# Three of six hidden pairs by seven products in each of chunks 3 to 6, with the sums placed early and one buffer for loaded values

## The chip, the cores and the metric

One core of a Trainium2 chip runs the whole program. The metric is the device time of one execution in microseconds. The kernel before takes 328.5 us (median of 3 runs, 328.02 to 328.99).

The profile names the engines PE (TensorE, matmuls), PEld (TensorE's weight loads), DVE (VectorE), ACT (ScalarE), POOL (GpSimd) and SP (SyncE, which here only issues transfers). The granted clock is the share of TensorE's full clock that the profile shows as allowed. A bank is one of the pieces of PSUM, the memory into which TensorE writes. An L and a number is a line of the kernel's source. The line numbers of the two kernels differ, so I pair lines by what they do.

## The reference, cut to what matters

```python
# attention over keys and values that are means of 8 neighbours: 8 batches, 8 heads, 576 rows, 64 columns
k_p = k.reshape(B, H, 72, 8, 64).mean(axis=3)
v_p = v.reshape(B, H, 72, 8, 64).mean(axis=3)
attn = softmax(q @ k_p.T / 8)
x = (attn @ v_p) as 4608 tokens x 512
# gated block
gate = maximum(x @ w_gate, 0)          # 512 -> 1536
out = (gate * (x @ w_val)) @ w_out     # 1536 -> 512
```

## The kernel before

The attention of batch c + 1 is woven between the products of chunk c of 512 tokens; there are nine chunks, 0 to 8. GpSimd adds up the means (the code calls these additions trees) two batches ahead, and issues the loads.

An ordinary hidden block computes 128 gates and 128 values for 512 tokens:

```python
def gate_val(c, fo, t0=0, n=TCH):          # 4 + 4 matmuls of 128x512
    ...
    nc.scalar.activation(out=relu[:, :n], in_=ps[0][:, :n], func=AF.Relu)
    nc.vector.tensor_tensor(out=h_tiles[c][:, fo, t0:t0 + n], in0=ps[1][:, :n], in1=relu[:, :n], op=ALU.mult)
```

Two such blocks, fo and fo + 6, and the two halves of the chunk form a 2 x 2 block product, which can be done with seven products instead of eight (28 matmuls of 256 columns instead of 16 of 512). The price is sums of weights, sums of inputs and more additions behind the products. The kernel before does this for two pairs of chunk 6, all six of chunk 7 and four of chunk 8. The output product already uses seven products in each chunk.

The parts on GpSimd that the argument touches:

```python
vin_pool = ctx.enter_context(tc.tile_pool(name="vin", bufs=2))

def prep_k(b, load_next, behind=None):
    for i in range(KJ // 2):
        run(pool_k(b, i, nc.gpsimd))                       # trees of keys
    if behind is not None:
        nc.gpsimd.tensor_copy(out=gate, in_=behind)        # holds the loads back
    if load_next:
        load_k(b + 1); load_q(b + 1); load_v(b + 1)

def prep_v(b):
    for g in range(NG):
        run(pool_v(b, g, nc.gpsimd))                       # trees of values
```

The queries are transposed by a DMA that SyncE issues when they have landed.

The softmax here doesn't subtract the row's maximum and nothing guards it: scores larger than these inputs give would overflow.

Of the kernel before, what the change touches and what calls it, by code (L numbers as in the profile page):

```python
# [16 lines left out]
def kernel(  # L17
# [13 lines left out]
    POOL = 8  # L31
# [15 lines left out]

    KP = 12
# [9 lines left out]
    vin_pool = ctx.enter_context(tc.tile_pool(name="vin", bufs=2))  # L58
    tree_pool = ctx.enter_context(tc.tile_pool(name="tree", bufs=2))
# [7 lines left out]
    relu_pool = ctx.enter_context(tc.tile_pool(name="relup", bufs=3))  # L67
    fout_pool = ctx.enter_context(tc.tile_pool(name="foutp", bufs=2))
    pexp_pool = ctx.enter_context(tc.tile_pool(name="pexpp", bufs=2))
# [19 lines left out]
    kg = const_pool.tile([P, QT * 2 // POOL, 2 * D], F16, name="kg")  # L89
    warm_sb = const_pool.tile([P, TCH], F16, name="warm_sb")  # L90


    stats = [const_pool.tile([P, NG, 4 * D], F16, name=f"stat{i}") for i in range(2)]
# [58 lines left out]
    def load_v_wide(b):  # L152
        tl = vin_pool.tile([P, H, POOL, D], F16, name="v_in")
        main = tl[:, :H // 2].rearrange("p h t d -> p (h t d)").rearrange(
            "p (h t d) -> p h t d", h=H, d=D)
        rest = tl[:P // 2, H // 2:].rearrange("p h t d -> p (h t) d")[:, :H]
        v_tiles[b] = (main, rest)
        nc.gpsimd.dma_start(
            out=main.rearrange("p h t d -> p h (t d)"),
            in_=v[b].rearrange("h (x t) d -> x h (t d)", t=KG)[:P])  # L160
        nc.gpsimd.dma_start(
            out=rest, in_=v[b].rearrange("h r d -> r h d")[P * KG:])
# [34 lines left out]
    def pool_v(b, g, eng):  # L197
        st = stats[b % 2][:SP, g, :].rearrange("p (x d) -> p x d", d=D)[:, 0::3, :]
        src = v_tiles[b][:SP, 2 * g:2 * g + 2].rearrange("p h t d -> p h (t d)")
        return tree(eng, SP, src, st)  # L200
# [135 lines left out]
    def pool_v_array(b, half):  # L336

        ps = ps_mm.tile([P, HH, D], F32, name="mm_ps", tag="mm_ps")
        main, rest = v_tiles[b]
        hs = slice(half * HH, (half + 1) * HH)  # L340
        for t in range(KG):
            nc.tensor.matmul(
                out=ps[:SP], lhsT=sel_main, rhs=main[:, hs, t, :], start=(t == 0), stop=False)
        nc.tensor.matmul(
            out=ps[:SP], lhsT=sel_rest[:P // 2], rhs=rest[:, hs, :], start=False, stop=True)
        g0 = half * NG // 2
        st = stats[b % 2][:SP, g0:g0 + NG // 2, :]
        st = st.rearrange("p g (x d) -> p g x d", d=D)[:, :, 0::3, :]
        src = ps[:SP].rearrange("p (g x) d -> p g x d", x=2)
        nc.scalar.copy(st, src)  # L350
# [6 lines left out]
    def piece_scores(t):  # L357
        n, j = divmod(t, 2)
        cols = [(j, n * IQ, IQ)] if n < NF else [(0, NF * IQ, RI), (1, NF * IQ, RI)]
        e = pexp_pool.tile([P, H, P], F16, name="pexp")  # L360
# [15 lines left out]
    def values(b, t):  # L376
# [6 lines left out]
        for half in range(2):  # L383
            ps = ps_at.tile([P, 512], F32, name="at_ps", tag="at_ps")
            for h in range(half * HH, (half + 1) * HH):
                g, hh = divmod(h, 2)
                c0 = g % (NG // 2) * W + hh * (D + 1)
                s0 = 3 * D - 1 if hh else 0
                nc.tensor.matmul(  # L389
                    out=ps[:n, c0:c0 + D + 1], lhsT=weights(b, h, t),  # L390
                    rhs=stats[b % 2][:SP, g, s0:s0 + D + 1], start=True, stop=True,
                )
# [73 lines left out]
    def out_rows(c, ts, eng=None):  # L466
# [3 lines left out]
        def part(lo, hi):  # L470
# [8 lines left out]
            if hi == n_fo:  # L479
                o = fout_pool.tile([P, DM], F32, name="fout")  # L480
# [13 lines left out]
    wo_sums = const_pool.tile([P, 4, n_hf, HD], F16, name="wo_sums")  # L494

    def weight_sums():
# [3 lines left out]
        t1, t2, t3, t4 = [wo_sums[:, i] for i in range(4)]  # L500
        return [lambda o=o, x=x, y=y, i=slice(i, i + 2): nc.vector.tensor_tensor(
                    out=o[:, i], in0=x[:, i], in1=y[:, i], op=ALU.subtract)
                for o, x, y in ((t1, f, e), (t2, h, t1), (t3, h, f), (t4, g, t2))
                for i in range(0, n_hf, 2)]

    def out_products(c, last=False):
# [5 lines left out]
        S = [sum_pool.tile([P, n_hf, HT], F16, name=f"sum{i}") for i in range(4)]  # L512
        e, g, h = wo_sb[:, :n_hf, :HD], wo_sb[:, n_hf:, :HD], wo_sb[:, n_hf:, HD:]
        T = [wo_sums[:, i] for i in range(4)]
# [72 lines left out]
    def last_products(c):  # L587
# [5 lines left out]
        S = [sum_pool.tile([P, n_hf, HT], F16, name=f"sum{i}").rearrange(  # L593
            "p f (z t) -> p f z t", z=2) for i in range(4)]
        e, g, h = wo_sb[:, :n_hf, :HD], wo_sb[:, n_hf:, :HD], wo_sb[:, n_hf:, HD:]
        T = [wo_sums[:, i] for i in range(4)]
# [83 lines left out]
    F_HALF = n_hf * P  # L680
    w_sums, x_sums, mids = {}, {}, {}

    def hidden_weight_sums():

        flat = [vin_pool.tile([P, H, POOL, D], F16, name="v_in").rearrange(
            "p h t d -> p (h t d)") for _ in range(2)]
        flat.append(kin_pool.tile([P, KJ, POOL, D], F16, name="k_in").rearrange(
            "p j t d -> p (j t d)"))
        n = N_CO * F_HALF
        views = [t[:, i * n:(i + 1) * n] for t in flat for i in range(2)]  # L690
        views += [q16_pool.tile([P, QT * D], F16, name="q16")[:, :n] for _ in range(2)]
        views = [t.rearrange("p (k f) -> p k f", k=N_CO) for t in views]
        w_sums[0], w_sums[1] = views[:4], views[4:]
        for f0 in range(0, F_HALF, 2 * P):
            fs, fu = slice(f0, f0 + 2 * P), slice(F_HALF + f0, F_HALF + f0 + 2 * P)
            for m, w in enumerate((wg_sb, wv_sb)):
                s1, s2, s3, s4 = [t[:, :, fs] for t in w_sums[m]]
                a11, a12 = w[:, :N_CO, fs], w[:, N_CO:, fs]
                a21, a22 = w[:, :N_CO, fu], w[:, N_CO:, fu]
                for o, x, y, op in ((s1, a21, a22, ALU.add), (s2, s1, a11, ALU.subtract),  # L700
                                    (s3, a11, a21, ALU.subtract), (s4, a12, s2, ALU.subtract)):
                    nc.gpsimd.tensor_tensor(out=o, in0=x, in1=y, op=op)

    def x_quarters(c):
        x0 = c * TCH % RING
        return [x_T[:, k * N_CO:(k + 1) * N_CO, x0 + t * HT:x0 + (t + 1) * HT]
                for k in range(2) for t in range(2)]

    def x_sums_of(c):

        e, f, g, h = x_quarters(c)
        x_sums[c] = [exp_pool.tile([P, 2, HS], F16, name="expT").rearrange(
            "p x s -> p (x s)")[:, :N_CO * HT].rearrange("p (k t) -> p k t", k=N_CO)
            for _ in range(4)]
# [5 lines left out]
    def take_mids():  # L720
# [4 lines left out]
        tiles += [fout_pool.tile([P, DM], F32, name="fout") for _ in range(2)]  # L725
# [3 lines left out]
    def hidden_products(c, fo, z):  # L729
# [28 lines left out]
        def summed(i):  # L758
            return lambda m: w_sums[m][i][:, :, fs]
# [56 lines left out]

    def hidden_round(c, fo, others, sums):
# [28 lines left out]
    def prep_k(b, load_next, behind=None):  # L846

        for i in range(KJ // 2):
            run(pool_k(b, i, nc.gpsimd))
        if behind is not None:  # L850
            nc.gpsimd.tensor_copy(out=gate, in_=behind)  # L851
        if load_next:
            load_k(b + 1)
            load_q(b + 1)
            load_v(b + 1)

    def prep_v(b):
        for g in range(NG):
            run(pool_v(b, g, nc.gpsimd))
# [10 lines left out]
    def attention(b):  # L870
# [10 lines left out]
        return [[kt]] + [[]] * (b + 1 < B) + trios + [[p] for p in V], []  # L881

# [7 lines left out]
    with tc.manual_schedule():  # L890
# [95 lines left out]
        load_v(2)  # L986

# [16 lines left out]
        prep_k(2, True)  # L1004
        prep_v(2)
# [4 lines left out]
        for c in range(1, n_chunks):  # L1010
            gv = [lambda fo=fo: gate_val(c, fo) for fo in range(n_fo)]

            if c == 1:
                sums = weight_sums()
                units = weave_units(gv[:-1], o[5:])
            elif c < C_HIDDEN:
                prods, sums = out_products(c - 1)
                units = []
                order = range(n_fo - 1)
                if c == C_HIDDEN - 1:  # L1020

                    order = [fo for fo in range(n_fo) if fo % n_hf > 1]
                for fo in order:
                    if c == C_HIDDEN - 1 and len(prods) == 2:
                        units.append(gv[fo])
                        continue
                    units.append(gv[fo])
                    if prods and fo not in (1, 4, 7, 10):
                        units.append(prods.pop(0))
# [31 lines left out]
            prep_v_at = 3  # L1061
            if c + 1 < B:
                others, later = attention(c + 1)
                if left:
                    others[1:2] = [[piece] for piece in left]
# [5 lines left out]
            for i, unit in enumerate(units):  # L1071
                if i == 3 and c + 2 < B:
                    prep_k(c + 2, c + 3 < B, h_tiles[c][:, 1, :1] if c > 1 else None)
                if i == prep_v_at and c + 2 < B:
                    prep_v(c + 2)
                unit()
                if c == 1:
                    run(sums[i:i + 1])
# [6 lines left out]
                if c == C_HIDDEN - 1 and i == 0:  # L1085
                    hidden_weight_sums()
                elif c == C_HIDDEN - 1 and i == 11:
                    run(x_sums_of(c))
            if c == C_HIDDEN - 1:
                take_mids()  # L1090
                more = x_sums_of(c + 1)
                run(hidden_round(c, 0, prods, sums[6:] + more[:2]) + more[2:])
            else:
                gv[-1]()
# [32 lines left out]
```

## Time and profile before

| what | before |
|---|---|
| time | 328.5 us |
| TensorE busy | 97% of the span |
| VectorE, GpSimd, ScalarE busy | 69%, 63%, 47% |
| a matmul of 512, of 256 columns, back to back | 0.216 us, 0.109 us |
| lost by TensorE over the span | 17.4 us: 9.5 before the second chunk, 3.8 in chunks 1 to 8, 4.1 behind them |

"Lost" in this document always means the same thing. I take how much later each matmul starts than the one before it, subtract the usual spacing for its width (216 ns for 512 columns, 123 for 288, 109 for 256, 56 for 128, 32 for 65 and so on), and add this up over a stretch. In contrast to "busy" it also counts time in which a matmul stands in the queue and seems to run. Stretches are cut where a chunk transposes its pooled keys, once a chunk. The lines of the profile of before are shown in the prediction.

### The profile page before, as it was taken

Reading aid. Unit: us, or ns where it says so; the run is one execution under the profiler, and the core shown is the slowest. Engines: PE = TensorE matmul, PEld = TensorE weight load, DVE = VectorE, ACT = ScalarE, POOL = GpSimd, SP = SyncE. Lnnn points to the kernel's source line nnn. Section 1 sums busy time; section 2 is a strip of 40 time slices with the busy share of each in tenths; the row PEclk is TensorE's granted clock in tenths of the full one; section 3 lists DMA queues with packets and bytes.
Section 4 is the critical chain, followed back from the end, with each engine's and each line's share of the span. In section 5 each row is a group of like instructions: output and inputs, shape, how many; then the busy total and the mean of one; then the engine's idle time right before and its main releaser. Section 6 shows DMA issues by size and latency. Waiting matters only on the chain.

```text
span 326.5 us, 6890 instructions
## 1 busy us (share of the span) xinstructions
PE 316.8 (97%) x2614; PEld 224.7 (69%) x2614; DVE 226.6 (69%) x482; ACT 151.9 (47%) x353; POOL 206.2 (63%) x258
## 2 busy tenths in 40 slices
PE   7899999999999999999999999999999999999995
PEld 2577885455566656665888866655667888888674
DVE  7465737677684864696387745784789989879762
ACT  1444482364466226612672257225925565565331
POOL 8556607999999942992199309999902577667300
PEclk9999999999999999999999999999999999999999
DMA  7999998996958539953694472123012220130044
GB/s 111 187 201 204 200 213 148 197 171 123 187 105 159 103 98 149 170 85 89 139 165 82 86 113 51 32 49 123 1 26 50 41 90 0 25 110 0 12 116 132
DMA packets 51009, 35.44 MB, mean 109 GB/s; under 512 B 30432, under 2 KB 45024, under 8 KB 50976
## 3 DMA queue, kind: packets, MB, share of 16 engines
q0 software_dynamic: 18304, 18.88, 35.8%
q1 hardware_dynamic: 32528, 16.00, 22.5%
q8 instruction: 20, 0.33, 0.4%
q10 hardware_dynamic: 144, 0.13, 0.1%
q14 instruction: 13, 0.11, 0.1%
HBM read 37.75 MB, written 9.44 MB: 145 GB/s over the span
## 4 chain that ended last, share of the span: by engine, by line
PE 88%; DVE 6%; DMA 2%; issue 1%; ACT 1%; POOL 1%; DVEq 0%; ACTq 0%; POOLq 0%
PE mm_ps L430 42%; PE acc_ps L530 19%; PE mm_ps L749 9%; PE at_ps L310 4%; PE mm_ps L475 3%; PE at_ps L389 3%; PE mm_ps L609 2%; PE at_ps L749 2%; DMA q<-in_q_dram 2%; DVE px L395 1%; DVE sum L521 1%; DVE h L439 1%; PE mm_ps L412 1%; DVE px L765 1%; PE mm_ps L284 1%
## 5 line engine op out<-in xcount | busy, mean ns | idle before, releaser
L439 DVE TENSOR_TENSOR h<-mm_ps,relu 128x512 f16<-128x512 f32 (+1 forms) x96 | 59.8, 624 | 68.2 <-PE mm_ps L430 55.2
L436 ACT ACTIVATE relu<-mm_ps 128x512 f16<-128x512 f32 (+1 forms) x96 | 52.2, 544 | 99.9 <-PE mm_ps L430 91.7
L430 PE MATMUL mm_ps<-x_T,wv_sb 128*128 128x512 f16 (+1 forms) x432 | 88.5, 332 | 0.3 <-DVE kpT0u L266 0.3
L430 PE MATMUL mm_ps<-x_T,wg_sb 128*128 128x512 f16 (+1 forms) x432 | 88.5, 332 | 0.0
L430 PEld LDWEIGHTS <-wv_sb 128*128 128x128 f16 x432 | 42.2, 98 | 31.1 <-DVE kpT0u L266 0.8
L430 PEld LDWEIGHTS <-wg_sb 128*128 128x128 f16 x432 | 40.0, 98 | 20.7 <-issue 0.4
L327 ACT ACTIVATE expT<-at_ps 72x288 f16<-72x288 f32 (+2 forms) x128 | 39.7, 384 | 13.4 <-PE at_ps L310 12.7
L530 PEld LDWEIGHTS <-sum 128*128 128x128 f16 x336 | 32.3, 98 | 6.8 <-DVE sum L521 1.2
L395 DVE TENSOR_TENSOR px<-at_ps,prd 128x256 f16<-128x256 f32 (+1 forms) x80 | 33.8, 423 | 2.7
L183 POOL TENSOR_TENSOR tree_b<-tree_a 72x256 f32<-72x256 f32 (+1 forms) x42 | 33.1, 789 | 3.3
L771 POOL TENSOR_TENSOR h<-px 128x256 f16<-128x256 f16 x36 | 25.5, 720 | 13.4 <-ACT px L768 12.3
L530 PE MATMUL acc_ps<-wo_sums,sum 128*128 128x256 f16 x252 | 31.0, 273 | 0.0
L177 POOL TENSOR_TENSOR tree_a<-v_in 72x512 f32<-72x512 f16 x24 | 28.7, 1194 | 0.1
L177 POOL TENSOR_TENSOR tree_a<-k_in 96x512 f32<-96x512 f16 x18 | 20.9, 1160 | 12.1 <-DMA k_in<-in_k_dram 12.1
L530 PEld LDWEIGHTS <-h 128*128 128x128 f16 x252 | 24.0, 98 | 3.0
L851 POOL COPY gate<-h 128x1 f16<-128x1 f16 x4 | 1.5, 381 | 36.8 <-DVE h L439 36.8
L770 POOL TENSOR_SCALAR px<-px 128x256 f16<-128x256 f16 x12 | 13.0, 1080 | 18.3 <-PE mm_ps L749 15.2
L530 PE MATMUL acc_ps<-wo_sb,h 128*128 128x256 f16 x168 | 20.6, 273 | 0.0
L521 DVE TENSOR_TENSOR sum<-h 128x768 f16<-128x768 f16 x28 | 19.3, 689 | 0.0
L538 DVE TENSOR_TENSOR rows<-acc_ps,mid 128x512 f32<-128x512 f32 x21 | 14.4, 686 | 4.8 <-PE acc_ps L530 4.6
L389 PEld LDWEIGHTS <-expT 72*128 72x128 f16 (+1 forms) x280 | 12.9, 100 | 5.9 <-DVE prd L394 0.8
L394 DVE RECIPROCAL prd<-at_ps 128x4 f32<-128x4 f32 (+1 forms) x80 | 13.7, 171 | 3.7 <-PE at_ps L389 3.6
(144 smaller groups left out, 520.2 us busy)
## 6 DMA issues: line engine op xcount, KB each, us to landing
out_dram<-rows SPq DMA_DIRECT2D x24, 256.0 KB
k_in<-in_k_dram POOLq DMA_DIRECT2D x7, 576.0 KB, 6.7
q<-in_q_dram POOLq DMA_DIRECT2D x7, 576.0 KB, 8.9
v_in<-in_v_dram POOLq DMA_DIRECT2D x6, 576.0 KB, 12.6
out_dram<-rows SPq DMA_DIRECT2D x14, 128.0 KB
wg_sb<-in_moe_w_gate_dram POOLq DMA_DIRECT2D x6, 256.0 KB, 11.4
wv_sb<-in_moe_w_val_dram POOLq DMA_DIRECT2D x6, 256.0 KB, 11.0
wo_sb<-in_moe_w_out_dram POOLq DMA_DIRECT2D x3, 512.0 KB, 10.1
```

The lines of the kernel that those rows point to most:

```text
L177: eng.tensor_tensor(out=cell["a"][:n], in0=src[:, :, :4 * D], in1=src[:, :, 4 * D:], op=ALU.add)
L183: eng.tensor_tensor(out=cell["c"][:n], in0=a[:n, :, :2 * D], in1=a[:n, :, 2 * D:], op=ALU.add)
L327: nc.scalar.activation(out=out_ap, in_=in_ap, func=AF.Exp, scale=EXP_SCALE)
L389: nc.tensor.matmul(out=ps[:n, c0:c0 + D + 1], lhsT=weights(b, h, t), rhs=stats[b % 2][:SP, g, s0:s0 + D + 1], start=True, stop=True,)
L395: nc.vector.tensor_tensor(out=x[:n, half * NG // 2:(half + 1) * NG // 2, :, :], in0=pv.rearrange("p g (x c) -> p g x c", x=2)[:, :, :, :D] ...
L430: nc.tensor.matmul(out=t[:, lo:hi], lhsT=w[:, ci, fsl], rhs=x_T[:, ci, x0:x0 + hi - lo], start=(ci == 0), stop=(ci == n_co - 1),)
L436: nc.scalar.activation(out=relu[:, :n], in_=ps[0][:, :n], func=AF.Relu)
L439: nc.vector.tensor_tensor(out=h_tiles[c][:, fo, t0:t0 + n], in0=ps[1][:, :n], in1=relu[:, :n], op=ALU.mult)
L521: nc.vector.tensor_tensor(out=S[k][:, i], in0=x[:, i], in1=y[:, i], op=op)
L530: nc.tensor.matmul(out=ps[:, tb, :], lhsT=lhs[:, i, tb * P:(tb + 1) * P], rhs=rhs[:, i, :], start=(first and tb == 0 and i == 0), stop=(tb ...
L749: nc.tensor.matmul(out=ps[key][:, m], lhsT=w_of(m)[:, i], rhs=xs[:, i], start=(first and m == 0 and i == 0), stop=(m == 1 and i == N_CO - ...
L771: nc.gpsimd.tensor_tensor(out=hc[:, fo_out, cols], in0=gv[:, 0], in1=gv[:, 1], op=ALU.mult)
```

## The change

Its intent is to take columns off TensorE: in chunks 3 to 6 three of the six pairs go by seven products, the first three of each chunk's pairs, all behind the values. Chunk 6 did two pairs so before, so ten pairs are new. The order of each chunk is now a written string. To make room for the sums of weights, values have one load buffer instead of two. The trees' intermediate tiles (one instead of two), the sums of the output product (three tiles instead of four) and the row buffers are shared more tightly as well; no run tests these apart, but a tree of keys starts every 2.44 us as before. The sums of the output product move to the beginning of a chunk. The diff is cut.

```diff
-    vin_pool = ctx.enter_context(tc.tile_pool(name="vin", bufs=2))
+    vin_pool = ctx.enter_context(tc.tile_pool(name="vin", bufs=1))
...
+    E_PAIRS = 3
+    C_EARLY = 3
+    def early_weight_sums():                 # six sums of 128x768 on GpSimd, ahead of chunk 1
...
+    EARLY_ORDER = """
+        X X g s S kt K o s S q g s a o s X a g s a o s X a g s s a
+        o a v g v o v T g v o v
+        x1 x5 y1 x2 x6 y5 x3 y2 x7 y6 z1 x4 y3 z5 y7 z2 z6 y4 z3 z7 o z4 W"""
...
+            elif key == "K":
+                if c == C_HIDDEN - 1:
+                    hidden_weight_sums()     # eight sums of 128x768 on GpSimd, in chunk 6
+                if c < C_EARLY:
+                    trees_k(b + 1)
+                    trees_v(b + 1)
+                if b + 2 < B:
+                    nc.gpsimd.tensor_copy(out=gate, in_=h_tiles[c][:, ...])
+                    load_k(b + 2); load_q(b + 2); load_v(b + 2)
+            elif key == "T":                 # trees of keys
+                trees_k(b + 2)
+            elif key == "W":                 # trees of values
+                trees_v(b + 2)
```

In the string, g is an ordinary block, o an output product, s a sum for it, X a sum of inputs, a three scores, v a piece of values, kt the transposes of pooled keys, q those of queries, S the sending of a result, and x1 to z7 the seven products of the three pairs. Behind each pair's products ScalarE takes relus and GpSimd makes the products of gate and value (three a pair, 128x256). T stands before the pairs, so the trees of keys stand ahead of these products in GpSimd's queue.

## The prediction

> **What bounds the kernel now.** First the page's engine totals:
>
> ```profile
> span 326.5 us, 6890 instructions
> PE 316.8 (97%) x2614; PEld 224.7 (69%) x2614; DVE 226.6 (69%) x482; ACT 151.9 (47%) x353; POOL 206.2 (63%) x258
> PEclk9999999999999999999999999999999999999999
> ```
>
> TensorE is busy nearly throughout at full granted clock. Busy is not the same as full speed, so I next read the chain of waits in order of time (start us, length us, what), in the fourth and sixth chunks of 512 tokens (chunks 3 and 5 in the code's count from 0):
>
> ```profile
> 131.47 1.73 PE mm_ps L430 x8
> 133.57 1.31 PE acc_ps L530 x12
> ...
> 216.39 1.39 DVE sum L521
> 217.79 0.60 DVE rows L538
> 218.39 0.84 DVE sum L521
> ```
>
> Eight matmuls of 512 columns take 1.73 us, 0.216 us each; twelve of 256 columns take 1.31 us, 0.109 us each. A column costs the same either way. Summing over the trace how much later each matmul starts than the usual spacing of its width allows, I find from 30 us to 303 us about 5.5 us of lost time (1.67 us to 58, 0.44 in chunk 1, 1.06 in chunk 2, 0.20, 0.24, 0.69 and 0.62 in chunks 3 to 6, 0.57 in chunk 7). So the kernel is bound by the number of columns streamed. What interrupts it is short: at 216 to 219 us the last product of the output waits for its sum on VectorE, and the same happens at 116 us.
>
> Next the windows, one a chunk for chunks 2 to 6, then chunk 7, which already computes all pairs by seven products (columns: window, length, busy us and instructions of each engine, clock, DMA share, GB/s):
>
> ```profile
> 82.00:118.80 36.80, 36.45 (x276) 22.30 (x273) 27.17 (x60) 16.41 (x35) 33.85 (x44) 1.00 0.70 128
> 118.80:152.40 33.60, 33.60 (x245) 20.93 (x243) 22.51 (x45) 14.81 (x32) 19.11 (x25) 1.00 0.69 121
> 152.40:186.30 33.90, 33.90 (x326) 28.84 (x324) 22.67 (x45) 14.80 (x32) 19.23 (x25) 1.00 0.61 120
> 186.30:220.30 34.00, 33.69 (x260) 22.28 (x259) 22.05 (x45) 14.80 (x32) 23.75 (x25) 1.00 0.35 66
> 220.30:255.20 34.90, 34.82 (x269) 23.17 (x267) 26.22 (x54) 18.59 (x54) 18.96 (x17) 1.00 0.18 47
> 255.20:303.00 47.80, 47.77 (x434) 42.24 (x433) 41.61 (x72) 28.52 (x66) 32.81 (x41) 1.00 0.15 45
> ```
>
> VectorE (third busy figure) has 11 us to spare in chunks 3 to 5, ScalarE 19 us, GpSimd 10 to 14 us. Chunk 7 shows that 87% of VectorE can be carried with little stall if the order suits.
>
> **What the Trainium skill says.** "Perfetto Trace Analysis", section "Identifying the Most-Contended Engine", warns that matmul busy time does not tell how near TensorE is to its limit; hence the spacing above. "TensorE: Matmul & The Clock Gate", section "Back-to-back issue gap", gives N/2.4 + 2.5 ns for an isolated gap, which this trace meets (216 and 109 ns), and 131 ns sustained at 512 columns, which it does not. "SBUF — State Buffer", section "SBUF: two separate sides", says that a VectorE operation with two SBUF inputs and a GpSimd operation that reads SBUF exclude each other for a whole instruction. The trace agrees: a 128x768 sum takes 0.55 us with GpSimd idle (124.7 us) and up to 1.98 us beside a tree (130.6 us).
>
> **The change part by part.**
>
> TensorE. A pair of hidden blocks (one of the first six and its partner), gate and value, is now 16 matmuls of 512 columns: 16 x 0.216 = 3.46 us. By seven products it is 28 of 256 columns: 28 x 0.109 = 3.05 us, so 0.41 us less a pair. Three pairs in each of chunks 3 to 6 are twelve, but two of chunk 6 were done so before: ten new pairs. The built programs confirm 444 instead of 556 matmuls of 512 columns and 1596 instead of 1412 of 256: 112 x 0.216 - 184 x 0.109 = 4.14 us less. (Chunk 4 wraps round the ring of inputs and already runs in 256-column halves, so its saving is real but made of other counts.) No other matmul count changes. This is all on the path: **-4.1 us**.
>
> VectorE, per pair: two products of 128x512 from PSUM (0.69 us each, 1.38) become three additions (0.68) and one product of 128x256 (0.42), 2.46 us; plus 1.08. Per chunk 3 x 1.08 and four input sums (0.42 to 0.89 each, say 2.3) make +5.5 us: 28 us of a chunk that should take 32.5, or 87%. This lies beside TensorE, but unevenly. Taking the new order row by row, everything before the pairs (six ordinary blocks 4.1, eight sums 6.3, input sums 2.3, five values of 1.2 each, four output additions 2.75) is 21.5 us of VectorE against 21.9 us of TensorE. With GpSimd's trees now beside the sums it can be 2 us more. I expect VectorE to be 2 to 3 us behind when the pairs begin, with the values waiting for their three banks.
>
> ScalarE, per pair: two relus of 0.60 become three copies of 0.59, three relus of 0.41 and one of 0.38: 3.4 us, so 10.1 us for three pairs against 10.5 us of TensorE in that stretch (21 products of 0.437 and one output product of 1.31). Locally that is full. The copies wait for four row buffers that VectorE's additions release, so VectorE's lag passes on. I estimate about 1 us of new stall per chunk where values and pairs follow each other, in four chunks: **+4 us**.
>
> GpSimd. Six sums of 128x768 come in before chunk 1. It has an idle hole there:
>
> ```profile
> 50.38 1.14 POOL L177 TENSOR_TENSOR tree_a<-k_in 96x512 f32<-96x512 f16 x1 [12.12 <-DMA k_in<-in_k_dram]
> ...
> 128.19 0.45 POOL L851 COPY gate<-h 128x1 f16<-128x1 f16 x1 [10.28 <-DVE h L439]
> ```
>
> From 0.72 us for 256 f16 elements and about 1.2 for 512, 768 should take about 1.7 us; six are 10.2 us, which fit into the 12.1 us. Later, each of chunks 3 to 6 gets nine products of 0.72, 6.5 us, within its spare time. In chunk 6 the 24 weight sums of about 1.2 us (29 us, spread over chunks 5 and 6) become eight of about 1.7 (14 us).
>
> One buffer for values instead of two: a load can only start after the trees of the batch before. The loads land 6 us (keys), 8 (queries) and 11 to 12 us (values) after the issue of the keys, so mostly it hides behind trees of keys (about 8 us). Following GpSimd with measured durations: trees of batch 4 end at 108 us instead of 110, then the loads of batch 5 land (114 us), trees of 5 to 132, loads of 6 land at 139, its key trees end at 146.5. The first of the nine products of chunk 3 is wanted at about 145 us and its buffer at 147. So chunk 3 may lose about 1 us there, **+1 us**. In chunk 4 the corresponding trees end at about the same time as the first product is ready.
>
> Sums early in a chunk remove the two waits at 117 and 218 us (0.5 us each), and interleaving takes some of the 0.62 us of chunk 6 and of chunk 2's 1.06: **-1.5 us**. Start and tail keep their products; their 7.8 and 4.1 us of gaps stay.
>
> Sum: 328.5 - 4.1 + 4 + 1 - 1.5 = 327.9. The two positive terms are my least certain; the order looks tuned, and any pause of TensorE lets VectorE catch up. I take 1 us off: **327.0 us**.
>
> **The rivals.**
>
> First, the column count decides alone: 324.4 us, and with the old waits gone, 323. For it: chunk 7 at 87% VectorE loses 0.57 us in 48 us. Against it: there the load is even, while here both VectorE and ScalarE are full in turns.
>
> Second, VectorE becomes the bound of chunks 3 to 6. If contention makes its sums 1.0 us on average, its 28 us become 30, and each chunk stays at 33.5 to 34.5 us: total 328 to 331. For it: sums of 1.3 to 2.0 us beside trees. Against it: 30 is still under 32.5.
>
> Third, the single value buffer or GpSimd's order (trees of keys ahead of the products, values behind) holds back the hidden blocks, and the next chunk's first sum and product wait: 3 to 6 us in chunk 3, perhaps again in chunk 4, total 330 to 335. For it: GpSimd is 92% busy in chunk 2 and has no double buffer left. Against it: its 10 us of waiting at the gate is slack before anything is late.
>
> Fourth, a gain beyond 2%, that is under 321.9 us: it needs the whole 4.1 us and 2.5 of the 5.5 us of old stalls with no new ones.
>
> **Range and chances.** The column saving is certain within 0.2 us. New stalls between nothing and twice my 5 us, less up to 1.5 us of old ones, give 322.9 to 332.9; I narrow the upper end a little: 323.0 to 332.0. Faster by over 2% (under 321.9) 0.05, slower by over 2% (over 335.1) 0.04, within 0.91.
>
> **What would show it.** TensorE's matmul spacings must stay 0.216 and 0.109 us, with 2686 matmuls. My steps are right if chunk 3 to 6 windows are 33 to 34 us each, VectorE is busy 27 to 30 us in each, values and pairs show gaps on TensorE ended by VectorE or ScalarE, and GpSimd's six early sums end before 51 us. Chunks of 32.3 us without gaps mean that rival one holds and my stall term was wrong. A wait of VectorE's additions or of the first sum of a chunk for GpSimd above 2 us means rival three. A changed start (before 30 us) or tail would be outside all this.

## The result, and the profile after

The changed kernel takes 342.84 us (median of 4 runs, 340.76 to 344.58) against 328.26 us of the kernel before beside it. The ratio is 1.0439, 95% interval 1.0369 to 1.051: slower by 4.4%, outside my range. A ratio here is the mean time of one kernel's fast runs over that of the other's of the same rounds, so not quite the ratio of the medians that I quote.

The engine totals of the page after:

```profile
span 340.0 us, 7128 instructions
PE 319.0 (94%) x2686; PEld 233.2 (69%) x2686; DVE 253.9 (75%) x517; ACT 170.9 (50%) x405; POOL 222.2 (65%) x275
PEclk9999999999999999999899999999999999999999
```

TensorE fell to 94% of a longer span, no other engine is near its limit, and in one slice of forty the granted clock is lower. So nothing became the bound as a whole; the loss must be local. The windows of chunks 3 to 6, cut at the chunks' own beginnings (columns as in the prediction):

```profile
123.65:164.55 40.90, 34.78 (x280) 25.33 (x279) 28.88 (x57) 19.52 (x45) 28.85 (x39) 0.96 0.75 125
164.55:198.85 34.30, 33.35 (x329) 29.18 (x328) 27.42 (x56) 20.21 (x47) 25.62 (x34) 1.00 0.75 118
198.85:233.15 34.30, 33.22 (x281) 24.48 (x280) 27.28 (x56) 20.21 (x47) 16.91 (x22) 1.00 0.37 67
233.15:270.40 37.25, 33.99 (x281) 24.46 (x280) 33.47 (x56) 21.64 (x63) 21.05 (x18) 1.00 0.20 45
```

Chunks 4 and 5 take 34.3 us, just above the 33 to 34 that I expected. Chunk 3 takes 40.9 and has the mean granted clock of 0.96; chunk 6 takes 37.25, with VectorE busy for 33.5 us in it instead of the 28 that I had worked out for an ordinary chunk of the four. Split by loss, in us:

| stretch | lost before | lost after | change |
|---|---|---|---|
| start to the second chunk | 9.51 | 10.46 | +0.95 |
| chunk 1 | 0.44 | 0.04 | -0.40 |
| chunk 2 | 1.06 | 2.09 | +1.03 |
| chunk 3 | 0.20 | 8.66 | +8.46 |
| chunk 4 | 0.24 | 1.99 | +1.75 |
| chunk 5 | 0.68 | 2.08 | +1.40 |
| chunks 6 to 8 | 1.20 | 5.53 | +4.33 |
| behind chunk 8 | 4.09 | 4.13 | +0.04 |

The changes add up to +17.6 us. The columns at their usual spacing fell from 307.93 to 303.80 us, that is by 4.13 us. The spans differ by 17.56 - 4.13 = 13.4 us (326.5 and 340.0). So the gain is there in full, and new stalls have eaten it four times over. There are three places: chunk 3, chunk 6, and about 1.5 us in each of chunks 4 and 5.

**Chunk 3.** The chain of waits in order of time (start, length, what) of the changed kernel, through that chunk:

```profile
144.12 6.27 DMA k_in<-in_k_dram
...
150.47 1.15 POOL tree_a L183
...
157.36 0.11 POOL kp L194
...
157.77 1.30 POOL h L893 x2
...
159.10 0.70 DVE relu L889
...
159.84 2.32 PE mm_ps L871 x11
```

Before, this stretch of the chain was nearly all TensorE's. Now the chain runs from a load of keys, through GpSimd's trees of them, to GpSimd's first product of a gate and a value (h), from there to an addition on VectorE, which waited 5.63 us for the relu buffer that this product frees, and only then to TensorE. TensorE's own line at the end of it (start, busy time, and in brackets the idle time before it and what ended it):

```profile
159.84 0.40 PE L871 MATMUL mm_ps<-early_x,wg_sb 128*128 128x256 f16 x2 [5.04 <-DVE relu L889]
```

The gap costs more than its 5 us. The windows behind it:

```profile
159.80:161.50 1.70, 1.66 (x9) 1.23 (x9) 0.92 (x2) 1.03 (x4) 1.15 (x2) 0.58 0.15 58
161.50:164.20 2.70, 2.70 (x18) 2.05 (x16) 1.48 (x3) 0.66 (x2) 1.96 (x3) 0.63 0.00 0
```

The granted clock is 0.58 and 0.63 over these 4.4 us: 1.70 x 0.42 + 2.70 x 0.37 = 1.7 us more, as an estimate. The two windows average over their edges: from 160.1 to 163.4 us alone the clock is 0.50. The Trainium skill, "TensorE: Matmul & The Clock Gate", section "HAM oscillation — how this bites in real kernels", names gaps over about 3.4 us as the ones to avoid because the clock falls. This trace agrees: after the 5 us gap the clock fell, while the gaps under 1 us elsewhere left it at 1.00. But a gap of that length is not needed. In the run below that reorders the pairs, the clock was 0.50 from 96.6 to 100.0 us, after three waits of 0.81, 0.28 and 0.49 us within 2.5 us.

Why GpSimd came so late shows on its own timeline, where the waits stand in brackets:

```profile
84.25 1.14 POOL L183 TENSOR_TENSOR tree_a<-v_in 72x512 f32<-72x512 f16 x1 [4.80 <-DMA v_in<-in_v_dram]
...
115.42 0.86 POOL L136 DMA_DIRECT2D v_in<-in_v_dram  x1
120.58 1.14 POOL L183 TENSOR_TENSOR tree_a<-k_in 96x512 f32<-96x512 f16 x1 [4.30 <-DMA k_in<-in_k_dram]
133.21 1.15 POOL L183 TENSOR_TENSOR tree_a<-v_in 72x512 f32<-72x512 f16 x1 [4.62 <-DMA v_in<-in_v_dram]
144.12 0.56 POOL L131 DMA_DIRECT2D k_in<-in_k_dram  x1
150.47 1.15 POOL L183 TENSOR_TENSOR tree_a<-k_in 96x512 f32<-96x512 f16 x1 [4.11 <-DMA k_in<-in_k_dram]
157.77 3.17 POOL L893 TENSOR_TENSOR h<-relu 128x256 f16<-128x256 f16 x5
```

Four waits for loads, all on one engine that works in order. Between the first and the second it does not pause, yet the gate before the loads of batch 5 comes at 114 us. I had expected 108. The values issued at 115.42 land at 133.1, 17.7 us later, although those of the kernel before took 12.4 (issued at 98.97, landed at 111.38). The five products at 157.77 run back to back; the first two of them held TensorE.

**Chunks 4 and 5.** The chain in chunk 5 of the changed kernel, cut:

```profile
217.43 0.25 PE at_ps L395 x8
...
224.61 1.90 DVE relu L889 x3
...
227.60 0.43 DVE h L926
```

The wait for a late sum, which stood in the chain before at 216 to 219 us, is gone. In its place VectorE's work for the pairs (L889 the addition of two products, L926 the product of a gate and a value) stands in the chain twice where the pairs begin.

**Chunk 6.** VectorE's sums for the output there (of the changed kernel; the pair of numbers at the front is start and busy time of both):

```profile
235.93 3.30 DVE L529 TENSOR_TENSOR sum<-h 128x768 f16<-128x768 f16 x2
239.75 3.31 DVE L529 TENSOR_TENSOR sum<-sum,h 128x768 f16<-128x768 f16 x2
```

That is 1.65 us for a sum that takes 0.55 alone. What GpSimd did at the same time:

```profile
235.08 1.82 POOL L732 TENSOR_TENSOR k_in<-wg_sb 128x768 f16<-128x768 f16 x1
...
238.77 1.96 POOL L732 TENSOR_TENSOR k_in<-wg_sb 128x768 f16<-128x768 f16 x1
```

The eight sums of weights for chunk 7 run one after another from there. So a sum on VectorE takes about as long as one of GpSimd's sums beside it. The prediction quotes the skill on such pairs of operations.

### The profile page after: what moved, and what is told of

The parts are those of the page before. It is cut to its first block, busy times and chain, and to the rows that moved or that the text cites. A ratio compares the mean times of both kernels' runs of the same rounds, so it can differ in the third digit from the quotient of the medians.

```text
span 340.0 us, 7128 instructions
## 1 busy us (share of the span) xinstructions
PE 319.0 (94%) x2686; PEld 233.2 (69%) x2686; DVE 253.9 (75%) x517; ACT 170.9 (50%) x405; POOL 222.2 (65%) x275
## 4 chain that ended last, share of the span: by engine, by line
PE 77%; DVE 10%; POOL 6%; DMA 4%; issue 1%; ACT 1%; POOLq 0%; DVEq 0%
PE mm_ps L436 29%; PE acc_ps L538 16%; PE mm_ps L783 8%; PE mm_ps L871 7%; PE at_ps L316 3%; PE mm_ps L481 3%; PE at_ps L395 2%; PE mm_ps L619 2%; DVE sum L529 2%; POOL tree_a L183 2%; DVE relu L889 2%; DMA k_in<-in_k_dram 2%; DMA q<-in_q_dram 2%; POOL tree_b L189 2%; DVE px L401 1%
## 5 line engine op out<-in xcount | busy, mean ns | idle before, releaser
L445 DVE TENSOR_TENSOR h<-mm_ps,relu 128x512 f16<-128x512 f32 (+1 forms) x76 | 45.8, 604 | 36.9 <-PE mm_ps L436 29.7
L442 ACT ACTIVATE relu<-mm_ps 128x512 f16<-128x512 f32 (+1 forms) x76 | 40.2, 530 | 64.6 <-PE mm_ps L436 55.9
L436 PE MATMUL mm_ps<-x_T,wg_sb 128*128 128x512 f16 (+1 forms) x328 | 67.9, 332 | 0.0
L436 PE MATMUL mm_ps<-x_T,wv_sb 128*128 128x512 f16 (+1 forms) x328 | 67.8, 332 | 0.0
L893 POOL TENSOR_TENSOR h<-relu 128x256 f16<-128x256 f16 x36 | 24.5, 697 | 38.4 <-ACT relu L892 38.4
L436 PEld LDWEIGHTS <-wv_sb 128*128 128x128 f16 x328 | 32.0, 98 | 23.7 <-DVE kpT0u L272 0.4
L885 ACT COPY row<-mm_ps 128x512 f32<-128x512 f32 x36 | 19.5, 589 | 15.4 <-PE mm_ps L871 15.4
L889 DVE TENSOR_TENSOR relu<-mm_ps,row 128x512 f16<-128x512 f32 x24 | 16.1, 686 | 10.1 <-POOL h L893 5.6
L538 PE MATMUL acc_ps<-wo_sb,sum 128*128 128x256 f16 x168 | 21.4, 278 | 1.7 <-DVE mid L546 0.9
L538 PE MATMUL acc_ps<-wo_sums,sum 128*128 128x256 f16 x168 | 20.8, 272 | 0.2 <-DVE sum L529 0.2
L538 PE MATMUL acc_ps<-wo_sb,h 128*128 128x256 f16 x168 | 20.6, 273 | 0.0
L395 PEld LDWEIGHTS <-expT 72*128 72x128 f16 (+1 forms) x280 | 13.4, 100 | 7.4 <-DVE px L401 1.1
```

The costliest lines, as they stand in the source:

```text
L436: nc.tensor.matmul(out=t[:, lo:hi], lhsT=w[:, ci, fsl], rhs=x_T[:, ci, x0:x0 + hi - lo], start=(ci == 0), stop=(ci == n_co - 1),)
L538: nc.tensor.matmul(out=ps[:, tb, :], lhsT=lhs[:, i, tb * P:(tb + 1) * P], rhs=rhs[:, i, :], start=(first and tb == 0 and i == 0), stop=(tb ...
L893: nc.gpsimd.tensor_tensor(out=hc[:, fo_out, cols], in0=gv[key][:, 0], in1=gv[key][:, 1], op=ALU.mult)
```

## The experiments

The theories: the order of GpSimd's queue (trees of keys ahead of the products of the pairs) makes the gap of chunk 3; against it, the late loads and the single buffer make it, whatever the order. The weight sums in chunk 6 make the second loss; against it, chunk 6 suffers from what came before. Every run computed the right result. Runs of one group shared a chip and the runs of the kernel before. Some executions of several variants were 2 to 6% slower than the fastest of the same kernel; they count as slow and are in no ratio.

### Trees of keys behind the pairs

```diff
-        o a v g v o v T g v o v
-        x1 x5 ... z3 z7 o z4 W
+        o a v g v o v g v o v
+        x1 x5 ... z3 z7 o z4 T W
```

> Only the order on GpSimd changes: in chunks 3 and 4 the trees of the keys stand behind the nine products of the pairs instead of ahead of them. Theory A (the products of chunk 3 wait in GpSimd's queue behind trees that themselves wait for a load): the 5.2 us gap of TensorE at 154.5 us and the low clock after it (0.58 to 0.63 from 159.8 to 164.2 us) go, chunk 3 loses about 2 us like chunks 4 and 5 instead of 8.7, and the time is 335 to 337.5 us against 342.8 for the changed kernel. Theory B (VectorE and ScalarE are too full where values and pairs meet, my step of +4 us): chunk 3 keeps most of its loss and the time stays above 340 us.

335.8 us median (fast runs 334.69, 335.88, 335.72; one slow of 341.63), ratio 1.0208 (1.0167 to 1.0249). Chunk 3 loses 2.44 us instead of 8.66, and the clock stays at 1.00. GpSimd in that stretch:

```profile
148.89 1.35 POOL L893 TENSOR_TENSOR h<-relu 128x256 f16<-128x256 f16 x2 [1.58 <-ACT relu L892]
...
159.18 1.33 POOL L183 TENSOR_TENSOR tree_a<-k_in 96x512 f32<-96x512 f16 x1
```

The first product now starts at 148.89, when its gate is there, and the trees come at 159.18. The loads are as late as before: GpSimd waited 7.33 us for values at 134.6. So the late load did no harm here, where no product stood behind it. The order is needed for the gap; that a late load is needed as well, the next runs ask. Chunks 6 to 8 still lose 5.53 us, so that loss has a cause of its own.

### Weight sums in chunk 5 instead of chunk 6

```diff
-                if c == C_HIDDEN - 1:
+                if c == C_HIDDEN - 2:
                     hidden_weight_sums()
```

> The eight sums of weights of 128x768 move on GpSimd from the start of chunk 6 to chunk 5, after the trees of batch 7, where GpSimd idles 12.9 us. If they stretch VectorE's sums in chunk 6 (sums of 0.55 us took 1.39 to 1.65 us there, and TensorE lost about 3.5 us between 242 and 253 us), that loss goes and the time falls by 2 to 4 us, to 339 to 341 us; chunk 5's products start up to 2.5 us late on GpSimd and may give 1 us back. If instead VectorE's own number of operations bounds chunk 6, the loss stays within 1 us of what it was.

The times are inconclusive: 336.02 and 339.07 fast, 353.03 and 348.46 slow; ratio of the fast ones 1.0273 (1.0201 to 1.0345). The trace of the fast 336.02 still says where things went. Chunks 6 to 8 lose 2.25 us instead of 5.53, and chunk 5 loses 3.72, which is 1.6 more. So the sums do cost something wherever they stand: half of what chunk 6 lost by them turns up in chunk 5. In this execution chunk 3 lost only 2.4 us, although its order of trees and its single buffer are those of the change. The values of batch 5 kept GpSimd waiting 0.80 us instead of 4.62, the trees of keys ended at 151.3 us instead of 157.8, and GpSimd then waited 0.82 us for the first gate. TensorE came 2 us later as well, because chunk 2 lost 5.2 us, about 1.7 of them by a granted clock of 0.50 from 96.3 to 99.7 us. So with the same program the gap of chunk 3 comes or stays away with the time at which the loads land.

### Loads between the trees

The order of the string stays as in the change (T ahead of the pairs); only the loads are moved ahead of the trees of values.

```diff
             if c < C_EARLY:
                 trees_k(b + 1)
-                trees_v(b + 1)
             if b + 2 < B:
                 nc.gpsimd.tensor_copy(out=gate, in_=h_tiles[c][:, ...])
-                load_k(b + 2); load_q(b + 2); load_v(b + 2)
+                load_k(b + 2); load_q(b + 2)
+                if c < C_EARLY:
+                    trees_v(b + 1)
+                load_v(b + 2)
```

> In chunk 2 the loads of keys and queries of batch 5 are issued between the trees of keys and of values of batch 4 instead of after both; the one buffer for values and the order of trees and products stay. If the late GpSimd comes from waits for loads (4.3, 4.6 and 4.1 us before 120.6, 133.2 and 150.5 us), the key trees of batch 6 end about 8 to 13 us earlier, before the first product is wanted, and the gap of chunk 3 goes as in the run with trees behind: 335 to 337.5 us. If only the order of trees before products matters, the gap stays at 4 us or more, 340 us or more.

339.51 us median, and a spread that decides nothing: 334.64 and 335.88 fast, 343.14 and 353.92 slow; ratio of the fast ones 1.0203 (1.015 to 1.0256). The profile fell into the slow execution of 343.14. It has no 5 us gap in chunk 3 (2.43 us lost), but TensorE waits 5.9 us for transposed queries in chunk 2. I give no weight to that wait, as only a slow execution shows it. A cleaner form of the same test follows below.

### The kernel before with one buffer for values

```diff
-    vin_pool = ctx.enter_context(tc.tile_pool(name="vin", bufs=2))
+    vin_pool = ctx.enter_context(tc.tile_pool(name="vin", bufs=1))
+    wsum_pool = ctx.enter_context(tc.tile_pool(name="wsum", bufs=1))   # for the weight sums
...
         if load_next:
             ...
-            load_v(b + 1)
...
     def prep_v(b):
         ... (trees of values)
+        if b + 1 < B:
+            load_v(b + 1)
```

> The kernel before with one buffer for loaded values instead of two (each load of values issued behind the trees of the batch before), nothing else. If the single buffer by itself makes GpSimd late: 331 us or more. If the kernel before has slack enough on GpSimd (10 to 13 us at its gate in chunks 3 and 4), the same within 1 us: 327.5 to 329.5 us.

329.83 us median (329.61 to 330.46), ratio 1.0044 (1.0006 to 1.0082): 1.4 us, a little more than the band in which the buffer is nearly free, and far less than the gap. Chunk 2 loses 2.93 us instead of 1.06. So the single buffer alone is worth about what I had put down for it (+1), but in chunk 2, where two matmuls at 118 to 119 us wait 1.58 and 0.62 us for VectorE. The opposite test, the changed kernel with two buffers, could not be built: 3.4 KB a partition of SBUF (the memory that the engines read) were missing. What share the buffer has inside the changed kernel stays open for that reason.

### Trees behind, and the weight sums divided

On top of the first experiment: the four sums of gate weights in chunk 5, the four of value weights in chunk 6 behind the fifth ordinary block (a new letter U), behind the sums of that chunk.

```diff
-        o a v g v o v g v o v
+        o a v g v o v U g v o v
...
-                if c == C_HIDDEN - 1:
-                    hidden_weight_sums()
+                if c == C_HIDDEN - 2:
+                    hidden_weight_sums([0])
...
+            elif key == "U":
+                if c == C_HIDDEN - 1:
+                    nc.gpsimd.tensor_copy(out=gate, in_=h_tiles[c][:, n_hf + E_PAIRS + 1, :1])
+                    hidden_weight_sums([1])
```

> The trees of keys and values behind the products of the pairs, as in the first experiment (335.8 us median, fast runs from 334.7 us), and besides the eight weight sums of GpSimd taken out of the stretch in which VectorE makes its sums in chunk 6: four in chunk 5 after the trees, four in chunk 6 behind the fifth ordinary block. If the two share what they read, the 3.3 us that chunk 6 lost beyond chunks 4 and 5 go and the sums there fall from 1.4 to 1.65 us to about 0.55: 331.5 to 333.5 us. If chunk 6 is slow for another reason, no change: 334.5 us or more.

The fast runs are 331.51, 331.97 and 331.68 us (slow: 338.5, 340.23, 341.62), ratio 1.0101 (1.0075 to 1.0128). From the first experiment's 1.0208 that is 1.07%, or 3.5 us. The profile fell into a slow execution, but its chunks 6 to 8 lose 2.26 us instead of 5.53, which is 3.3 us less and agrees with the fast times. The next run, which divides the sums in the same way, has a fast profile and shows the sums themselves.

### The order within the pairs

On top of that: x7 before y2, and one product of the third pair takes its bank from another pool, so that VectorE adds up x7 before y2.

```diff
-        x1 x5 y1 x2 x6 y5 x3 y2 x7 y6 z1 ...
+        x1 x5 y1 x2 x6 y5 x3 x7 y2 y6 z1 ...
...
-            product("c", summed(0), x_sums[c][0], ps_mm)
+            product("c", summed(0), x_sums[c][0], *((ps_at, "at") if fo == 2 else (ps_mm, "mm")))
```

> The same as the run before it, and the two waits inside the three pairs are taken away: the seventh product of the first pair stands before the second of the second pair (its addition then ends before the fourth product wants the bank: gap of 0.47 us), and the fifth product of the third pair takes a bank of the values instead of the one that the fourth product of the first pair still holds (gap of 0.66 us). If these gaps are the cost of the pairs in each of chunks 3 to 6, 4 times 1.1 us go: 327 to 329.5 us. If VectorE or ScalarE is simply full there, the gaps come back at later products and at most 1.5 us go: 330.5 us or more.

328.36 us median (330.88, 328.43, 328.29, 327.4), ratio 1.001 (0.9966 to 1.0055), which is 0.9% or 3.0 us less than the run before it. Chunks 3, 4 and 5 lose 1.33, 1.04 and 1.34 us; in the first experiment, which has a fast profile and the old order of the pairs, they lost 2.44, 1.98 and 2.32. Where the pairs begin in chunk 5, two matmuls start 0.47 and 0.66 us late in the changed kernel, one behind an addition and one behind a product on VectorE; here one is left that starts 0.27 us late. So about 1 us a chunk came from the order in which the pairs want VectorE and the banks.

Chunks 6 to 8 lose 1.27 us. The sums of chunk 6 on VectorE, which took 3.30 us in the changed kernel:

```profile
229.36 1.01 DVE L529 TENSOR_TENSOR sum<-h 128x768 f16<-128x768 f16 x2
...
232.55 1.02 DVE L529 TENSOR_TENSOR sum<-sum,h 128x768 f16<-128x768 f16 x2
```

GpSimd begins its weight sums of that chunk at 244.5 us, behind the gate, and the pair of sums takes 1.01 us. The profiled execution is the longest of the four (330.88), and chunk 2 loses 4.75 us in it; about 1.7 of them are the clock of 0.50 named above.

### Loads between the trees, the values of batch 3 later

```diff
         if load_next:
             ...
-            load_v(b + 1)
+            if b != 2: load_v(b + 1)      # the values of batch 3 are loaded behind the trees of its keys
```

(on top of "Loads between the trees")

> Against the run with loads between trees, whose four executions went from 334.6 to 353.9 us: the load of the values of batch 3 is issued behind the trees of the keys of batch 3 (about 78 us) instead of at 69.3 us, where it met the transposes of the queries on the DMA engines (issued at 70.0 us[...]). If that meeting makes the late loads and the spread, all executions lie between 334.5 and 337 us and chunk 2 loses under 2.5 us. If the spread comes from elsewhere, one of the executions is above 340 us.

336.21 us, and the four runs lie within 0.2 us (336.14 to 336.33), ratio 1.0238 (1.0221 to 1.0255). The profile is of a fast execution, and chunk 2 loses 2.46 us in it. Chunk 3 loses 3.44 us, with no gap over 0.66 us, though T stands ahead of the pairs: GpSimd ends these trees at 147.8 us and then waits 2.83 us for the first gate. So the loads decide as well: the order alone does not make the gap. Both together do, and removing either one removes it.

What the load of these values met shows on two timelines. In the changed kernel, GpSimd issues it here and first uses it at 84.25, in the line shown above:

```profile
69.72 0.89 POOL L136 DMA_DIRECT2D v_in<-in_v_dram  x1
```

SyncE of the changed kernel issues the transposes of queries at the same moment:

```profile
69.86 4.54 SPq L300 DMA_TRANSPOSE qT<-q  x1
```

In this experiment, where the transposes are issued at 69.19:

```profile
76.59 0.89 POOL L136 DMA_DIRECT2D v_in<-in_v_dram  x1
83.76 1.14 POOL L183 TENSOR_TENSOR tree_a<-v_in 72x512 f32<-72x512 f16 x1 [5.20 <-DMA v_in<-in_v_dram]
```

The load takes 7.1 us instead of 14.5 and lands at nearly the same time (83.7 and 84.2): issued together with the transposes it gained nothing, in this place. The Trainium skill, "DMA: Bandwidth & Descriptors", section "Rules for kernel authors", says that transfers issued by different engines run on the same 16 DMA engines and interleave. That agrees with these two figures. The mechanism has not been isolated.

### The values of batch 3 later, alone

The same edit on the changed kernel, with nothing else.

> The changed kernel with the load of the values of batch 3 alone moved behind the trees of its keys, so that it no longer meets the transposes of the queries at 69 us. If that meeting costs what the changed kernel loses over the run with trees behind products (342.8 against 335.8 us), 335 to 337 us. If the order on GpSimd and the later waits for loads cost it, chunk 3 keeps a gap of 3 us or more and the time is 339 to 342 us, with a narrower spread.

342.7 us (341.44 to 343.56), ratio 1.0447 (1.0425 to 1.0468): no change. Chunk 3 loses 9.15 us, with a gap of 5.9 us before the same matmul. The values of batch 3 land at 83.5 us, so no tree starts earlier, and those of batch 5, issued at 114.6, land at 132.6 and are waited for again for 5 us. So the meeting at 70 us is not what makes the gap of chunk 3. It made no difference to the time here.

### All of it

Trees behind, weight sums divided, order of the pairs, loads between, values of batch 3 later.

> All of these together: trees behind products, weight sums away from VectorE's sums, the pairs' order and bank, loads between trees, the values of batch 3 later. If each removes its own loss, 326 to 329 us with a spread under 2 us, within 1% of the kernel before (328.1 us); the 4.1 us of columns saved are then taken up by the remaining stalls at the values (0.3 to 0.4 us a chunk) and in chunk 2.

329.15 us median (326.72 to 329.2), ratio 1.0004 (0.9967 to 1.0042). This cannot be told apart from the version without the last two. Chunk 3 loses 2.33 us instead of 1.33: once the trees stand behind the pairs, bringing the loads forward was of no use here.

### The last sum behind the values

The version with the pairs reordered, the values of batch 3 later, and the last sum of a chunk moved from before the values to behind the first products (in both strings).

```diff
-        X X g s S kt K o s S q g s a o s X a g s a o s X a g s s a
+        X X g s S kt K o s S q g s a o s X a g s a o s X a g s a
...
-        x1 x5 y1 x2 x6 y5 x3 x7 y2 ...
+        x1 x5 y1 s x2 x6 y5 x3 x7 y2 ...
```

> All repairs except the loads between trees (with them chunk 3 lost 0.32 and 0.66 us at 132 to 133 us, where VectorE's sums stood beside trees), and the last sum of a chunk moved behind the values, where the banks of the values made TensorE wait 0.32 to 0.44 us a chunk. If VectorE's lag at the values makes those waits, they go and the time is 325 to 327.5 us, with a spread under 2 us, 0.3 to 1% under the kernel before. If the lag only moves into the pairs, 327.5 to 329 us, the same as before.

326.68 us median of six runs (326.43 to 326.98) against 328.33 (eleven runs), ratio 0.995 (0.9937 to 0.9964). This beats both kernels, by 0.5% over the kernel before. Its page:

```profile
span 325.0 us, 7123 instructions
PE 314.9 (97%) x2686; PEld 232.4 (71%) x2686; DVE 244.6 (75%) x517; ACT 170.6 (52%) x405; POOL 220.7 (68%) x276
```

It runs the same 2686 matmuls as the changed kernel. Chunks 2 to 5 lose 1.23, 1.32, 0.99 and 1.08 us, 4.62 in all against 2.18 in the kernel before. Of the 4.13 us of columns this eats 2.4, and the span is 1.5 us shorter. Two edits separate this run from the one that reorders the pairs, so I do not divide the gain between them.

## Why the prediction was right or wrong

The prediction was 327.0 us in a range of 323 to 332, with 0.91 on "within 2%". The kernel took 342.84. It was wrong.

**What held.** The columns: -4.14 us worked out, -4.13 measured, with 2686 matmuls at the old spacings. The six sums of weights fit into the early hole of GpSimd. VectorE takes 27 to 29 us in chunks 3 to 5. The wait in the chain at 216 us is gone. The stall that VectorE's and ScalarE's work at the pairs causes was there, too: I put +1 us a chunk, and chunks 4 and 5 lost 1.75 and 1.40 us more. Here the mechanism was right, as the reordering of the pairs shows (it gave back about 1 us a chunk), and the term was mis-sized: 1.4 to 1.75 us a chunk instead of 1. With the other two losses taken away, chunk 3 lost 2.2 us more than in the kernel before (trees behind the pairs) and chunks 6 to 8 1.05 more (weight sums in chunk 5). That is 6.4 us over the four chunks where I had put 4.

**The step that failed: "One buffer for values instead of two", "+1 us".** I followed GpSimd with the landing times of the kernel before and got 146.5 us for the end of the key trees of batch 6, with the products wanted at 145. Measured: 157.8 us, with the first product wanted at 149.9, when ScalarE's relu for it ends. Of the 11 us, 6 had arisen by the gate before the loads of batch 5 (114 us instead of 108). GpSimd waited 4.80 us there for values which the one buffer had let it ask for only at 69.7 us; in the kernel before these trees started without a wait at 79.6. Another 4.6 us were the wait for the values of batch 5, which I had taken to be hidden behind the trees of keys. The products of the first pair then stood behind trees of keys, TensorE stood still for 5 us, and the clock fell: 8.5 us in chunk 3. My third rival described this ("The single value buffer or GpSimd's order"), and its size for chunk 3 (3 to 6 us) is that of the gap without the clock. I set it aside because of the slack at the gate. But the four waits for loads, of 4 to 5 us each on one in-order engine, two of which I had not counted, had used that slack up before the pairs of chunk 3. The experiments show that both parts are needed: with the trees behind the pairs the late loads do no harm, and with the loads moved the trees may stand ahead.

**The step that was missing: chunk 6.** I counted its weight sums as relief (29 us of GpSimd become 14). But in the same prediction I quoted that a VectorE operation and a GpSimd operation on SBUF exclude each other. The change puts both the sums of the output and the eight weight sums at the beginning of chunk 6. The sums went from 0.55 to 1.65 us, and chunks 6 to 8 lost 4.3 us more. With the weight sums divided, or in chunk 5, 3.3 us of it went away there. My second rival had this effect with 1.0 us a sum, spread over four chunks; it was 1.65, in one place.

**The term that fell short: "-1.5 us" for old stalls.** The late sums no longer wait, but chunk 2 loses 1.03 us more rather than less. The kernel before with one buffer loses 1.9 us more in chunk 2 as well, but at other places: its two long waits are at 118 to 119 us, while the late matmuls of the changed kernel are at 94.2 (0.69 us, behind ScalarE), 104.4 and 108.4 us (0.39 and 0.33, behind VectorE). So the cause of this loss is not shown. The +0.95 us before the second chunk I do not count as an effect: runs of versions with the same start lost between 9.4 and 10.5 us there.

**What stays open.** What share each neighbour has in the 17.7 us of the values of batch 5. They landed as SyncE was through with transposing queries (issued from 124.1 us on, for 9.1 us). The other traces sort by what the same load met. Issued right behind the keys and queries and landed before those transposes began, it took 13.8 and 13.2 us (weight sums in chunk 5, pairs reordered). Where the transposes began before it landed, it took 16.8 to 20.6 us (four versions, the changed kernel among them). Issued 10 us behind the keys and queries, and landed about when the transposes began, it took 7.7 us (loads between the trees, the values of batch 3 later). That fits both neighbours as causes, but these versions differ in other things too. Open is also why some versions have slow executions of 338 to 354 us on some chips. Of the six versions that issue the values of batch 3 together with the transposes (the changed kernel among them), 8 of 26 executions were slow; of the four that issue them later, none of 18. In both slow executions that were profiled TensorE waited in chunk 2 for transposed queries, 5.9 and 7.4 us. This points to that meeting of transfers, but the two runs that differ by it alone, one with slow executions and one without, were on different chips.

## What to carry to other kernels

Before hanging time-critical work on an engine with spare time, write down what stands ahead of it in that engine's queue and which transfer each of those waits for. The busy share says nothing about that, and with a buffer gone the landing times of the old kernel no longer hold. When operations are moved to an earlier place, look also at what the engine that shares their reads is doing at that place. And take a saving of columns as an upper bound: even the repaired order keeps only 1.6 of the 4.1 us.

## What the Trainium skill lacked or had wrong

- "DMA: Bandwidth & Descriptors" says that transfers share the DMA engines and interleave, but the skill gives no figure for a plain load beside DMA transposes. Here a load of values took 7.1 us beside none and 14.5 us when issued together with the transposes of queries.
- "SBUF — State Buffer" has the lock between VectorE and GpSimd; the slowing agrees with it, but the prediction's "the trace agrees" goes too far for a whole instruction. Side by side, 128x768 sums on VectorE took 1.65 us instead of 0.55 and one chunk lost over 3 us. GpSimd's sums of the same size took 1.70 to 1.96 us and started 1.88 us apart, against 1.64 us alone. One whole sum of each in turn would take about 2.1 us (an estimate, 1.64 + 0.50). The page gives no durations for two such streams of sums.
- "TensorE: Matmul & The Clock Gate" gives 131 ns for a sustained matmul of 512 columns; here it is 216 ns throughout, which is what its formula for an isolated matmul gives. It has no figure for several short waits in a row: here three waits of 0.28 to 0.81 us within 2.5 us were followed by 3.4 us at a clock of 0.50.
